# A fused attention and expert kernel on one core: ranks counted back from use in the last part, its last two units interleaved, and early loads planned late

## The chip, the cores and the metric

The kernel runs on one core of one Trainium2 chip. Five engines take part, each with its own queue, worked off in program order: TensorE (PE, with its weight loads shown as PEld), VectorE (DVE), ScalarE (ACT), GpSimd (POOL) and SyncE (SP), which here only issues DMAs. The metric is the device time of one execution in microseconds. It is compared with the median of repeated executions; the profile is that of one execution.

## The reference

```
x = attention(q, k, v)     # 4 batches, 8 heads, 576 positions, 64 wide; scores masked:
                           # heads 0-3 to the last 32 positions, heads 4-7 to every 32nd
x = x.transpose(0, 2, 1, 3).reshape(2304, 512)
p = domain_probs / (domain_probs.sum(-1, keepdims=True) + 1e-9)
for e in range(4):
    h = maximum(x @ w1[e], 0)              # (2304,512) @ (512,1024)
    out += p[:, e:e+1] * (h @ w2[e])       # (2304,1024) @ (1024,512)
```

All arrays are float32.

## The kernel before

**Three parts.** The 2304 rows of x are worked on in three parts of 384, 896 and 1024 rows. The first part runs together with the attention: TensorE takes the small attention products and the expert products of the first 384 rows by turns. The second part (896 rows) and the third (1024 rows) run alone behind it. Each part goes through eight units (four experts, two halves of 512 hidden columns each).

**The precision.** Each float32 operand of an expert product is kept as a high and a low half (`hi`, written by ScalarE; `lo`, the difference, written by VectorE or GpSimd), and each product of two such operands is three matmuls. Every operation here that reads a PSUM bank is VectorE's or ScalarE's.

**The third part.** A unit multiplies in Strassen's manner: 7 products of half-sized blocks for the hidden layer ("h") and 7 for the output ("o"), called P1, P2, s1, s2, s3, s4 and a22. One task, such as "h s2" or "o P1", is a pair of products (two halves f = 0, 1 of the rows of the result, each six matmuls of 128x512 in one PSUM bank, `product`, L897). In `plan_h` the products P1, s2, s3 and a22 accumulate one after the other in the same two ps banks, and s1 and s4 in two mo banks; after each step VectorE reads the bank (`finish`: an add at L928, a relu-and-scale by the expert's probabilities at L931) or ScalarE does (`park`, L919), before the next product may add to it. In `plan_t` the results q are combined (`sub`, L960) and split into halves (`put`: L955 high, L956 low) as the operands of the outputs: b11, t1, t2, b22, t3, b21 and t4 for "o P1", "o s1", "o s2", "o s4", "o s3", "o P2" and "o a22". In `plan_o` P1, s2, s3 and a22 accumulate in two sc banks, s1 and s4 in mo, P2 in ps, and VectorE adds every bank to the sums `acc` (L1005) before the next product goes on in it. Every unit runs through

```
TURN = ("h P1", "h s4", "h s2", "next P2", "h s3", "next s1", "h a22",
        "o P1", "o s1", "o s2", "o s4", "o s3", "o P2", "o a22")
```

where "next" is the hidden product of the unit behind it. Units come in the order 6, 0, 1, 2, 3, 4, 5, 7. The weights of the hidden products come back from DRAM with `reload` (L1033), those of the outputs with `plan_ring` (L983) into a ring of four buffers, all on SP's queue.

**The planner.** `Plan` takes every operation with its engine, its estimated duration, its dependencies and a rank (`prio`, an estimated time). `walk` simulates the engines and writes the program order: whichever engine can start first takes, among the operations that are ready on it, the one of the smallest rank. The expert products (`moe`) keep the order in which they were added; "VP" operations may go to VectorE or GpSimd and "AD" ones to ScalarE or VectorE, wherever they end first. `took` lengthens an operation with two SBUF operands on VectorE by up to half of GpSimd's remaining time. Loads go to SP with a planned wire: each occupies it for its `xfer` time, and `when` says how early an operation may start. Up to 45 us the planner puts idle matmuls (L1205) into gaps. The plan only fixes each engine's order; on the chip every operation waits for its semaphores alone.

The loads of the first part are q and k of a pair of heads (`load_qk`, L418 and L420), v (`load_v`, L425), and the expert weights w1 and w2, one buffer each (`load_w`, L634). A pair's loads are ranked by the planned time of the pair, the weights' by that of their unit; from the fifth pair on they are not planned earlier than 11 us before their use.

Of the kernel before, what the change touches and what calls it, by code (L numbers as in the profile page):

```python
# [11 lines left out]
AF = mybir.ActivationFunctionType  # L12
# [20 lines left out]
class Plan:  # L33
# [5 lines left out]
    TICK = 4096 / 1200  # L39
    BUSY, WARM = 3200, 2000  # L40
    LANES, RING = 8, 2048
    ROW = 2.0
    ENGINES = ("PE", "ACT", "DVE", "POOL", "SP")
    FLEX = {"VP": ("DVE", "POOL"), "AD": ("ACT", "DVE")}
# [59 lines left out]
    def walk(self):  # L104
# [57 lines left out]

        def when(o):
            t = o.ready
            if o.bank:
                n = len(allocs[o.bank[0]]) - self.banks[o.bank[0]]
                if n >= 0:
                    for p in self.readers.get(allocs[o.bank[0]][n], ()):
                        if p.start is None:
                            return None  # L170
                        t = max(t, p.end + self.SYNC)
            return t
# [134 lines left out]
def attn_moe_kernel(  # L307
# [13 lines left out]
    nc = tc.nc  # L321
# [84 lines left out]
    def engine(e):  # L406
        return nc.vector if e == "DVE" else nc.gpsimd
# [498 lines left out]
    DD = TH2 / 960 + 0.15  # L906
    rcnt = [0]

    def plan_h(u, step, z, dz):

        a, b, kk, first_in = STEPS[step]
        PARK = {"P2": "P2", "s1": "k1", "s4": "k2"}
        DONE = {"P1": (0, 0, "P2"), "s2": (0, 1, "k2"), "s3": (1, 1, "k1"), "a22": (1, 0, None)}

        def park(f, key, zz):
            i = ucnt[0] % 6
            ucnt[0] += 1
            late[PARK[step], f] = i
            add("ACT", TH2 / 1200 + 0.18, lambda: nc.scalar.activation(out=late["u"][i], in_=held[key][:, 0:TH2], func=AF.Copy),  # L919
                [key, "late3"], [f"u{i}"], zz)  # L920

        def finish(r, c, nm, f, key, zz):
            tok = f"q{r}{c}{f}"
            q = lambda: late["q"][r, c, f]
            src = lambda: held[key][:, 0:TH2]
            if nm:
                i = late[nm, f]
                add("DVE", DD, lambda: nc.vector.tensor_tensor(out=q(), in0=src(), in1=late["u"][i], op=ALU.add),  # L928
                    [key, f"u{i}", "late3"], [tok], zz)
            from_q = bool(nm)  # L930
            add("DVE", DD, lambda: nc.vector.scalar_tensor_tensor(  # L931
                out=q(), in0=q() if from_q else src(), scalar=0.0, in1=late["p"][:, c * TH2:c * TH2 + TH2], op0=ALU.max, op1=ALU.mult),
                ["pb", "late3"] + ([] if nm else [key]), [tok], zz + 0.1, two=from_q)

        for f in range(2):
            key = ({"a": "ps", "b": "mo", "c": "mo"}[kk], "h" + kk, u, f)
            need = [a + "h", a + "l"] + [f"{b}{h}{j}" for h in "hl" for j in range(2)]
            add("PE", dz, lambda f=f, key=key: product(wq[a], xq[b], f, key, first_in, TH2),
                need, [key], z + f * dz, key if first_in else None, True, 6 * TH2)
            ze = z + f * dz + dz  # L940
            if step in PARK:
                park(f, key, ze)
            else:
                r, c, nm = DONE[step]
                finish(r, c, nm, f, key, ze)

    def plan_t(step, z, dz):


        q = {(r, c, j): (lambda r=r, c=c, j=j: late["q"][r, c, j], f"q{r}{c}{j}") for r in range(2) for c in range(2) for j in range(2)}  # L950

        def put(v, nm, j, zz):
            src, tok = v
            hi, lo = (lambda: late["T"][nm][0][j]), (lambda: late["T"][nm][1][j])
            add("ACT", TH2 / 1200 + 0.17, lambda: nc.scalar.activation(out=hi(), in_=src(), func=AF.Copy), [tok, "late3"], [f"T{nm}h{j}"], zz)  # L955
            add("VP", VP, lambda e: engine(e).tensor_tensor(out=lo(), in0=src(), in1=hi().bitcast(F32), op=ALU.subtract),  # L956
                [tok, f"T{nm}h{j}"], [f"T{nm}l{j}"], zz)

        def sub(dst, a, b, zz):
            add("VP", VP, lambda e: engine(e).tensor_tensor(out=dst[0](), in0=a[0](), in1=b[0](), op=ALU.subtract), [a[1], b[1]], [dst[1]], zz)  # L960

        for j in range(2):
            if step == "P1":
                put(q[0, 0, j], "b11", j, z)
            elif step == "s2":
                sub(q[0, 0, j], q[0, 1, j], q[0, 0, j], z)
                put(q[0, 0, j], "t1", j, z)
            elif step == "s3":
                sub(q[0, 0, j], q[1, 1, j], q[0, 0, j], z)
                put(q[0, 0, j], "t2", j, z)  # L970
                put(q[1, 1, j], "b22", j, z + 2 * dz)
                sub(q[0, 1, j], q[1, 1, j], q[0, 1, j], z + 4 * dz)
                put(q[0, 1, j], "t3", j, z + 4 * dz)
            else:
                put(q[1, 0, j], "b21", j, z + 2 * dz)
                sub(q[1, 0, j], q[1, 0, j], q[0, 0, j], z + 4 * dz)
                put(q[1, 0, j], "t4", j, z + 4 * dz)

    def plan_ring(u, step, z):
        i = rcnt[0] % RING  # L980
# [4 lines left out]
        return i  # L985

    acc_count = {}

    def plan_o(u, step, slot, first, last, z, dz):
        a, b, kk, first_in = STEPS[step]  # L990
        r, c = {"P1": (0, 0), "P2": (0, 0), "s1": (1, 1), "s3": (1, 1), "s2": (0, 1), "s4": (0, 1), "a22": (1, 0)}[step]
        for f in range(2):
            key = ({"a": "sc", "b": "ps", "c": "mo"}[kk], "o" + kk, u, f)
            zz = z + f * dz
            need = [f"ring{slot}"] + [f"T{b}{h}{j}" for h in "hl" for j in range(2)]
            add("PE", dz, lambda f=f, key=key: product(
                [late["ring"][slot][:, :, h] for h in range(2)], late["T"][b], f, key, first_in, TH2),
                need, [key], zz, key if first_in else None, True, 6 * TH2)
            i = (2 * r + f) * 2 + c
            tok = [f"acc{i}0"] if i < TBS[1] // P - 1 else [f"acc{i}{x}" for x in (0, DM // 2)]  # L1000
            n = acc_count[i] = acc_count.get(i, 0) + 1
            if n == 1:
                add("AD", ad(TH2), lambda e, i=i, key=key: copy(e, lambda: acc[i], key, lambda pt: pt[:, 0:TH2]), [key], tok, zz + dz)
            else:
                add("DVE", DD, lambda i=i, key=key: nc.vector.tensor_tensor(  # L1005
                    out=acc[i], in0=held[key][:, 0:TH2], in1=acc[i], op=ALU.add), [key], tok, zz + dz)
            if n == NU * (1 if (r, c) == (1, 0) else 2):
                add("SP", 0.4, lambda i=i, f=f: nc.sync.dma_start(
                    out=out_t[(2 * r + f) * P:(2 * r + f) * P + P, c * TH2:c * TH2 + TH2], in_=acc[i]), tok, [f"out{i}"],
                    zz + dz, xfer=((0.8, 128),))  # L1010
# [11 lines left out]
    def plan_second():  # L1022
# [1 line left out]
        zz = z  # L1024
        seq = second_order
        plan_p(seq[0], zz)
        for step in ("P2", "s1"):
            plan_h(seq[0], step, zz, dz)
            zz += 2 * dz

        def reload(step, v, z):
            nm = STEPS[step][0]
            add("SP", 0.4, lambda: nc.sync.dma_start(out=wt[nm].bitcast(F32), in_=d1[v, nm]), [f"d1{v}{nm}"], [nm + "h", nm + "l"],  # L1033
                z, xfer=((1.45, 128),))

        if NU > 1:
            reload("P2", seq[1], zz)
            reload("s1", seq[1], zz)
        for i, u in enumerate(seq):
            v = seq[i + 1] if i + 1 < NU else None  # L1040
            w = seq[i + 2] if i + 2 < NU else None
            slots = {}
            fetch = list(FETCH)
            for _ in range(RING):
                st = fetch.pop(0)
                slots[st] = plan_ring(u, st, zz)
            for what in TURN:
                kind, step = what.split()
                if kind == "next":
                    if v is None:  # L1050
                        continue
                    plan_h(v, step, zz, dz)
                    if w is not None:
                        reload(step, w, zz + 6 * dz)
                elif kind == "h":
                    plan_h(u, step, zz, dz)
                    if step in ("P1", "s2", "s3", "a22"):
                        plan_t(step, zz + 2 * dz, dz)
                    if v is not None:
                        reload(step, v, zz + 6 * dz)  # L1060
                    if step == "a22" and v is not None and units[v][0] != units[u][0]:
                        plan_p(v, zz + 4 * dz)
                else:
                    plan_o(u, step, slots[step], i == 0, i == NU - 1, zz, dz)
                    if fetch:
                        st = fetch.pop(0)
                        slots[st] = plan_ring(u, st, zz)
                zz += 2 * dz

    ucnt = [0, 0]  # L1070

# [222 lines left out]
```

## Time and profile before

| | |
|---|---|
| median of 3 runs | 824.32 us (823.99 to 825.2) |
| the profiled execution | 825.78 us |
| its span, first to last instruction | 824.0 us |
| mean granted clock of TensorE | 0.995 |
| busy: PE, PEld, DVE, ACT, POOL | 810.3, 686.0, 625.2, 330.6, 308.3 us |
| mean DMA rate | 205 GB/s |

Times in rows count from the start of the span. "Busy" of an engine is the time that its instructions cover; a matmul's own time overlaps the next one's, so of PE the start to start matters. The granted clock is 1.00 at 2.4 GHz and 0.50 at 1.2 GHz. A figure in brackets behind a row is the idle time of the engine just ahead of it, with what released it; "issue" means that the trace shows nothing that was waited for.

### The profile page before, as it was taken

The numbers are of one execution on the slowest core, as the hardware profiler recorded it, in microseconds if no ns is written. First come the engines' busy times: TensorE is split into PE (matmuls) and PEld (weight loads), VectorE is DVE, ScalarE is ACT, GpSimd is POOL, SyncE is SP. The second block draws the span as 40 slices with busy tenths as digits, with TensorE's granted clock in tenths as the row PEclk, the third lists the DMA queues.
The fourth block names the chain that finished last, engine by engine and source line by source line (L and its number), as shares of the span: only waits on it lengthen the run. The fifth ranks groups of instructions, "written<-read, shape, count | busy, mean of one in ns | idle before, by whom it ended". The sixth has DMA issues, their size and how long they took to land.

```text
span 824.0 us, 13898 instructions
## 1 busy us (share of the span) xinstructions
PE 810.3 (98%) x5385; PEld 686.0 (83%) x5388; DVE 625.2 (76%) x892; ACT 330.6 (40%) x616; POOL 308.3 (37%) x243
## 2 busy tenths in 40 slices
PE   8999999999999999999999999999999999999987
PEld 6888888999889888888989888887878787878765
DVE  6877867865588776868677693959796979788886
ACT  4643556444336353543535352524142323323140
POOL 5431332934173542515344270305050505142352
PEclk9999999999999999999999999999999999999998
DMA  9685532339578686867753405747474556635714
GB/s 336 218 312 183 204 138 83 102 125 330 211 256 283 258 307 236 324 212 293 260 205 128 175 30 180 278 157 249 148 251 172 188 211 173 232 125 204 208 48 153
DMA packets 70401, 168.69 MB, mean 205 GB/s; under 512 B 5152, under 2 KB 22720, under 8 KB 70336
## 3 DMA queue, kind: packets, MB, share of 16 engines
q1 hardware_dynamic: 70192, 167.73, 57.5%
q8 instruction: 42, 0.69, 0.3%
q14 instruction: 23, 0.19, 0.1%
q10 hardware_dynamic: 144, 0.08, 0.1%
HBM read 108.00 MB, written 59.79 MB: 204 GB/s over the span
## 4 chain that ended last, share of the span: by engine, by line
PE 95%; DVE 1%; DMA 1%; issue 1%; POOL 1%; ACT 0%; POOLq 0%; ACTq 0%
PE mo L897 21%; PE mo L750 17%; PE ps L897 16%; PE sc L897 15%; PE mo L734 8%; PE ps L750 5%; PE sc L750 5%; PE ps L561 2%; PE sc L479 1%; PE ps L533 1%; PE sc L474 1%; DMA qkL<-in_qk_local 1%; PE ps L569 1%; POOL q L960 1%; PE mo L1205 1%
## 5 line engine op out<-in xcount | busy, mean ns | idle before, releaser
L960 POOL TENSOR_TENSOR q<-q,q 128x512 f32<-128x512 f32 x31 | 44.8, 1445 | 211.9 <-DVE q L931 186.2
L750 PE MATMUL mo<-w2t,h 128*128 128x512 f32 x336 | 80.8, 389 | 0.0
L750 PEld LDWEIGHTS mo<-w2t,h 128*128 128x128 f32 x336 | 63.1, 188 | 13.0
L750 PE MATMUL mo<-w2t,hs 128*128 128x512 f32 x288 | 69.9, 395 | 0.0
L750 PEld LDWEIGHTS mo<-w2t,hs 128*128 128x128 f32 x288 | 53.0, 188 | 11.0
L741 DVE SCALAR_TENSOR_TENSOR h<-c,h 128x448 fp32r<-128x448 f32 x48 | 59.6, 1268 | 2.4 <-ACT h L738 1.0
L645 POOL TENSOR_TENSOR a<-raw,a 128x512 fp32r<-128x512 f32 x22 | 34.1, 1549 | 59.6 <-DVE c L1097 44.9
L644 ACT ACTIVATE w2t<-raw 128x512 fp32r<-128x512 f32 x60 | 36.8, 629 | 37.8 <-PE mo L750 24.7
L1005 DVE TENSOR_TENSOR acc<-sc,acc 128x512 f32<-128x512 f32 x58 | 38.7, 684 | 16.4 <-PE sc L897 15.8
L759 DVE SCALAR_TENSOR_TENSOR acc<-mo,pr,acc 128x512 f32<-128x512 f32 x45 | 33.6, 747 | 22.8 <-PE mo L750 22.5
L928 DVE TENSOR_TENSOR q<-ps,v 128x512 f32<-128x512 f32 x48 | 33.1, 689 | 20.6 <-PE ps L897 20.5
L919 ACT ACTIVATE v<-mo 128x512 f32<-128x512 f32 x48 | 28.7, 598 | 49.5 <-PE mo L897 47.9
L645 POOL TENSOR_TENSOR w2t<-raw,w2t 128x512 fp32r<-128x512 f32 x21 | 30.2, 1447 | 46.6 <-ACT w2t L644 44.0
L734 PE MATMUL mo<-xh,a 128*128 128x384 f32 x192 | 46.7, 345 | 0.0
L955 ACT ACTIVATE Tb11h<-q 128x512 fp32r<-128x512 f32 x16 | 10.0, 627 | 84.5 <-DVE q L931 84.5
L644 ACT ACTIVATE wv<-tmp 128x512 fp32r<-128x512 f32 x32 | 20.1, 631 | 58.0 <-POOL tmp L652 12.8
L931 DVE SCALAR_TENSOR_TENSOR q<-q,pb 128x512 f32<-128x512 f32 x48 | 41.1, 857 | 1.1
L750 PE MATMUL ps<-w2t,h 128*128 128x512 f32 x168 | 40.4, 389 | 0.0
L750 PE MATMUL sc<-w2t,h 128*128 128x512 f32 x168 | 40.4, 389 | 0.0
L645 DVE TENSOR_TENSOR w2t<-raw,w2t 128x512 fp32r<-128x512 f32 x39 | 33.9, 897 | 4.5 <-ACT w2t L644 4.5
L750 PEld LDWEIGHTS sc<-w2t,h 128*128 128x128 f32 x168 | 31.5, 188 | 6.5
L750 PEld LDWEIGHTS ps<-w2t,h 128*128 128x128 f32 x168 | 31.5, 188 | 6.5
(261 smaller groups left out, 2108.0 us busy)
## 6 DMA issues: line engine op xcount, KB each, us to landing
raw<-in_w SPq DMA_DIRECT2D x30, 1024.0 KB, 5.9
qkS<-in_qk_strided SPq DMA_DIRECT2D x16, 329.0 KB, 7.9
vstL<-in_v_local SPq DMA_DIRECT2D x8, 640.0 KB, 8.7
out<-acc SPq DMA_DIRECT2D x18, 256.0 KB, 2.0
vstS<-in_v_strided SPq DMA_DIRECT2D x8, 384.0 KB, 8.7
qkL<-in_qk_local SPq DMA_DIRECT2D x8, 336.0 KB, 6.8
pb<-dp SPq DMA_DIRECT2D x5, 512.0 KB, 6.9
qkL<-in_qk_local SPq DMA_DIRECT2D x8, 272.0 KB, 7.6
```

What stands on the lines that cost most here:

```text
L644: add("ACT", 0.62, lambda: nc.scalar.activation(out=hi(), in_=src(), func=AF.Copy), need, [name + "h"], z)
L645: add("VP", VP, lambda e: engine(e).tensor_tensor(out=lo(), in0=src(), in1=hi().bitcast(F32), op=ALU.subtract), need + [name + "h"], [name ...
L734: nc.tensor.matmul(pt[:, 0:TA], w[:, c % 2, (f % 2) * P:(f % 2) * P + P], (xl if i == 1 else xh)[c], start=j == 0, stop=j == 11)
L741: nc.vector.scalar_tensor_tensor(out=dst(), in0=src(), scalar=0.0, in1=hi().bitcast(F32), op0=ALU.max, op1=ALU.subtract)
L750: nc.tensor.matmul(pt, ht[f][:, ts], wt[f][:, cs], start=j == 0, stop=j == 11)
L759: nc.vector.scalar_tensor_tensor(out=a, in0=pt, scalar=sc, in1=a, op0=ALU.mult, op1=ALU.add)
L897: nc.tensor.matmul(pt, a[i == 2][:, j, f * P:f * P + P], b[i == 1][j][:, 0:TH], start=bool(first) and n == 0, stop=True, skip_group_check= ...
L919: add("ACT", TH2 / 1200 + 0.18, lambda: nc.scalar.activation(out=late["u"][i], in_=held[key][:, 0:TH2], func=AF.Copy), [key, "late3"], [f" ...
L928: add("DVE", DD, lambda: nc.vector.tensor_tensor(out=q(), in0=src(), in1=late["u"][i], op=ALU.add), [key, f"u{i}", "late3"], [tok], zz)
L931: add("DVE", DD, lambda: nc.vector.scalar_tensor_tensor(out=q(), in0=q() if from_q else src(), scalar=0.0, in1=late["p"][:, c * TH2:c * TH ...
L960: add("VP", VP, lambda e: engine(e).tensor_tensor(out=dst[0](), in0=a[0](), in1=b[0](), op=ALU.subtract), [a[1], b[1]], [dst[1]], zz)
L1005: add("DVE", DD, lambda i=i, key=key: nc.vector.tensor_tensor(out=acc[i], in0=held[key][:, 0:TH2], in1=acc[i], op=ALU.add), [key], tok, zz ...
```

## The change

Four things change, all of them in the order that is planned.

In `when`, a transfer that is not planned yet may not start before the planned wire is within DEEP = 1.5 us of being free, as long as the wire stands under 200 us.

In the third part, all tasks of all units are now listed first, and the planned time of every task is kept in `due`. The ranks of `finish`, `put`, `sub` and of the adds to `acc` are counted back from the task that needs their result, instead of on from the task that made it.

Three output tasks of the last unit but one are taken out of their place and put among the hidden tasks of the last unit: "o s3" ahead of its "h s3", "o P2" and "o a22" ahead of its "h a22". For these three, the products of kind b (P2) use mo banks instead of ps.

The ring's loads are planned four output tasks ahead over the whole list, where before every unit planned its first four at its start.

```diff
+    DEEP = 1.5
...
         def when(o):
             t = o.ready
+            if o.xfer is not None and o.start is None and wire < 200:
+                t = max(t, wire - self.DEEP)
...
-                    [key, f"u{i}", "late3"], [tok], zz)
+                    [key, f"u{i}", "late3"], [tok], min(zz, zs) - 0.8)
...
-                ["pb", "late3"] + ([] if nm else [key]), [tok], zz + 0.1, two=from_q)
+                ["pb", "late3"] + ([] if nm else [key]), [tok], zs if nm else min(zz, zs), two=from_q)
...
-                finish(r, c, nm, f, key, ze)
+                after = {"P1": "s2", "s2": "s3", "s3": "a22"}.get(step)
+                use, ops = {"P1": ("P1", 2), "s2": ("s1", 3), "s3": ("s2", 3), "a22": ("P2", 2)}[step]
+                finish(r, c, nm, f, key, due["h", after] + f * dz if after else ze + 4 * dz, due["o", use] - 1.5 - 0.8 * ops - 0.8 + 0.7 * f)
...
-    def plan_t(step, z, dz):
+    def plan_t(step, due):
 ...
-            add("ACT", TH2 / 1200 + 0.17, lambda: nc.scalar.activation(out=hi(), in_=src(), func=AF.Copy), [tok, "late3"], [f"T{nm}h{j}"], zz)
+            add("ACT", TH2 / 1200 + 0.17, lambda: nc.scalar.activation(out=hi(), in_=src(), func=AF.Copy), [tok, "late3"], [f"T{nm}h{j}"], zz - 1.6)
...
-                [tok, f"T{nm}h{j}"], [f"T{nm}l{j}"], zz)
+                [tok, f"T{nm}h{j}"], [f"T{nm}l{j}"], zz - 0.8)
...
+            add("VP", VP, lambda e: engine(e).tensor_tensor(out=dst[0](), in0=a[0](), in1=b[0](), op=ALU.subtract), [a[1], b[1]], [dst[1]], zz - 2.4)
...
+            z = {s: due["o", s] - 1.5 + 0.7 * j for s in STEPS}
...
             elif step == "s3":
-                sub(q[0, 0, j], q[1, 1, j], q[0, 0, j], z)
-                put(q[0, 0, j], "t2", j, z)
-                put(q[1, 1, j], "b22", j, z + 2 * dz)
-                sub(q[0, 1, j], q[1, 1, j], q[0, 1, j], z + 4 * dz)
-                put(q[0, 1, j], "t3", j, z + 4 * dz)
+                sub(q[0, 0, j], q[1, 1, j], q[0, 0, j], z["s2"])
+                put(q[0, 0, j], "t2", j, z["s2"])
+                put(q[1, 1, j], "b22", j, z["s4"])
+                sub(q[0, 1, j], q[1, 1, j], q[0, 1, j], z["s3"])
+                put(q[0, 1, j], "t3", j, z["s3"])
...
+    tags = {"a": "sc", "b": "ps", "c": "mo"}
...
+            after = {"P1": "s2", "s2": "s3", "s3": "a22", "s1": "s4"}.get(step)
+            zd = (due["o", after] + f * dz if after else zz + 5 * dz) - 0.8
...
-                    out=acc[i], in0=held[key][:, 0:TH2], in1=acc[i], op=ALU.add), [key], tok, zz + dz)
+                    out=acc[i], in0=held[key][:, 0:TH2], in1=acc[i], op=ALU.add), [key], tok, zd)
...
+        tasks = [("next", -1, "P2"), ("next", -1, "s1")]
+        for i in range(NU):
             for what in TURN:
                 kind, step = what.split()
...
+                tasks.append((kind, i, step))
+        tasks = [t for t in tasks if t[0] != "next" or t[1] + 1 < NU]
+        late_o = [("o", NU - 2, step) for step in ("s3", "P2", "a22")]
+        tasks = [t for t in tasks if t not in late_o]
+        for t, before in zip(late_o, (("h", NU - 1, "s3"), ("h", NU - 1, "a22"), ("h", NU - 1, "a22"))):
+            tasks.insert(tasks.index(before), t)
+        os = [t for t in tasks if t[0] == "o"]
+        due = [{} for _ in range(NU)]
+        for n, (kind, i, step) in enumerate(tasks):
+            due[i + (kind == "next")][kind[0] if kind != "next" else "h", step] = zz + 2 * dz * n
+        slots = {t: plan_ring(seq[t[1]], t[2], zz) for t in os[:RING]}
+        for t in tasks:
+            kind, i, step = t
+            if kind == "o":
+                tags["b"] = "mo" if t in late_o else "ps"
+                plan_o(seq[i], step, slots[t], i == 0, i == NU - 1, zz, dz, due[i])
+                n = os.index(t) + RING
+                if n < len(os):
+                    slots[os[n]] = plan_ring(seq[os[n][1]], os[n][2], zz)
...
+            zz += 2 * dz
```

The other steps of `plan_t` change as s3 does. The lines for "h" and "next" keep `plan_h`, `plan_t`, `reload` and `plan_p` as they were, with `due` passed on.

## Rows read from the trace of the kernel before

**Rows 1.** The page's first part: busy us, share, instructions of each engine.

```profile
PE 810.3 (98%) x5385; PEld 686.0 (83%) x5388; DVE 625.2 (76%) x892; ACT 330.6 (40%) x616; POOL 308.3 (37%) x243
```

**Rows 2.** Busy time in stretches: stretch, length, engines, granted clock, DMA share, GB/s.

```profile
0.00:40.00 40.00, 36.74 (x696) 28.86 (x700) 30.21 (x72) 21.28 (x48) 20.93 (x34) 1.00 0.77 274
...
60.00:66.00 6.00, 5.52 (x50) 5.26 (x50) 3.07 (x8) 1.65 (x4) 1.08 (x2) 0.72 0.29 116
...
503.34:544.42 41.08, 41.08 (x182) 33.72 (x181) 28.62 (x37) 17.00 (x30) 7.97 (x5) 1.00 0.68 236
544.42:773.24 228.82, 227.40 (x986) 183.79 (x985) 191.12 (x245) 72.36 (x122) 71.98 (x48) 1.00 0.56 194
773.24:820.24 47.00, 43.28 (x181) 34.39 (x179) 35.05 (x48) 9.46 (x16) 15.56 (x10) 0.96 0.36 120
```

**Rows 3.** The chain of waits from 484 us on: start, length, what.

```profile
571.78 0.24 issue
572.01 3.00 PE sc L897 x12
...
580.74 2.72 PE ps L897 x12
583.46 2.72 PE sc L897 x12
...
767.00 0.24 issue
...
804.79 4.56 PE sc L897 x12
```

**Rows 4.** Timeline of all engines, 567 to 578 us: start, length, engine, line.

```profile
570.63 0.68 DVE L931 SCALAR_TENSOR_TENSOR q<-ps,pb 128x512 f32<-128x512 f32 x1
...
571.24 1.27 DVE L1005 TENSOR_TENSOR acc<-sc,acc 128x512 f32<-128x512 f32 x2
...
572.01 0.70 PE L897 MATMUL sc<-Tt2h,ring 128*128 128x512 f32 x2 [0.24 <-issue]
...
572.43 1.35 DVE L956 TENSOR_TENSOR Tb21l<-q,Tb21h 128x512 fp32r<-128x512 f32 x1
...
573.70 0.68 DVE L1005 TENSOR_TENSOR acc<-mo,acc 128x512 f32<-128x512 f32 x1
...
574.30 1.39 DVE L956 TENSOR_TENSOR Tt4l<-q,Tt4h 128x512 fp32r<-128x512 f32 x1
...
575.62 0.68 DVE L1005 TENSOR_TENSOR acc<-mo,acc 128x512 f32<-128x512 f32 x1
...
576.35 0.30 PEld L897 LDWEIGHTS mo<-Tb22h,ring 128*128 128x128 f32 x2 [0.40 <-DVE acc L1005]
```

**Rows 5.** Timeline of all engines, 770 to 824 us.

```profile
795.46 0.73 PE L897 MATMUL ps<-t4h,a 128*128 128x512 f32 x2 [1.52 <-DVE q L928]
...
802.28 1.80 DVE L956 TENSOR_TENSOR Tt2l<-q,Tt2h 128x512 fp32r<-128x512 f32 x1 [1.18 <-ACT Tt2h L955]
...
804.01 0.68 DVE L1005 TENSOR_TENSOR acc<-sc,acc 128x512 f32<-128x512 f32 x1
...
804.79 0.78 PE L897 MATMUL sc<-Tt2h,ring 128*128 128x512 f32 x2 [2.18 <-issue]
```

**Rows 6.** Busy time in stretches of 2 us, columns as in rows 2.

```profile
806.00:808.00 2.00, 2.00 (x6) 1.54 (x6) 2.00 (x4) 0.00 (x0) 1.92 (x2) 0.50 0.00 0
```

**Rows 7.** Instructions of one line: count, then minimum, median and maximum in ns.

```profile
L960 DVE TENSOR_TENSOR q<-q,q x33: 678/694/1779, 517.7 to 806.9; 128x512 f32<-128x512 f32 x33
L960 POOL TENSOR_TENSOR q<-q,q x31: 1283/1295/1752, 523.1 to 807.0; 128x512 f32<-128x512 f32 x31
...
L1005 DVE TENSOR_TENSOR acc<-sc,acc x58: 673/691/693, 540.3 to 820.3; 128x512 f32<-128x512 f32 x58
```

**Rows 8.** SP's timeline up to 230 us: start, length of issue, line.

```profile
10.92 0.38 SPq L634 DMA_DIRECT2D raw<-in_w  x1
```

**Rows 9.** SP's waits, 48 to 70 us: who for whom, total, times, longest.

```profile
SPq L634 <- DVE pmS L488: 13.5, 1, 13.5
```

More of the change, by code (lines that the diff above doesn't have):

```diff
@@ L907, in attn_moe_kernel, with plan_h @@
     rcnt = [0]
-    def plan_h(u, step, z, dz):
+    def plan_h(u, step, z, dz, due):
         a, b, kk, first_in = STEPS[step]
@@ L920, in park, with finish @@
                 [key, "late3"], [f"u{i}"], zz)
-        def finish(r, c, nm, f, key, zz):
+        def finish(r, c, nm, f, key, zz, zs):
             tok = f"q{r}{c}{f}"
@@ L959, in sub @@
         def sub(dst, a, b, zz):
-            add("VP", VP, lambda e: engine(e).tensor_tensor(out=dst[0](), in0=a[0](), in1=b[0](), op=ALU.subtract), [a[1], b[1]], [dst[1]], zz)
+            add("VP", VP, lambda e: engine(e).tensor_tensor(out=dst[0](), in0=a[0](), in1=b[0](), op=ALU.subtract), [a[1], b[1]], [dst[1]], zz - 2.4)
         for j in range(2):
+            z = {s: due["o", s] - 1.5 + 0.7 * j for s in STEPS}
             if step == "P1":
-                put(q[0, 0, j], "b11", j, z)
+                put(q[0, 0, j], "b11", j, z["P1"])
@@ L965, in plan_t @@
             elif step == "s2":
-                sub(q[0, 0, j], q[0, 1, j], q[0, 0, j], z)
-                put(q[0, 0, j], "t1", j, z)
+                sub(q[0, 0, j], q[0, 1, j], q[0, 0, j], z["s1"])
+                put(q[0, 0, j], "t1", j, z["s1"])
             elif step == "s3":
-                sub(q[0, 0, j], q[1, 1, j], q[0, 0, j], z)
-                put(q[0, 0, j], "t2", j, z)
-                put(q[1, 1, j], "b22", j, z + 2 * dz)
-                sub(q[0, 1, j], q[1, 1, j], q[0, 1, j], z + 4 * dz)
@@ L973, in plan_t @@
-                put(q[0, 1, j], "t3", j, z + 4 * dz)
-            else:
-                put(q[1, 0, j], "b21", j, z + 2 * dz)
-                sub(q[1, 0, j], q[1, 0, j], q[0, 0, j], z + 4 * dz)
-                put(q[1, 0, j], "t4", j, z + 4 * dz)
+                sub(q[0, 0, j], q[1, 1, j], q[0, 0, j], z["s2"])
[3 more added lines that the diff above has]
+                put(q[0, 1, j], "t3", j, z["s3"])
+            else:
+                put(q[1, 0, j], "b21", j, z["P2"])
+                sub(q[1, 0, j], q[1, 0, j], q[0, 0, j], z["a22"])
+                put(q[1, 0, j], "t4", j, z["a22"])
@@ L987, in attn_moe_kernel, with plan_o @@
     acc_count = {}
-    def plan_o(u, step, slot, first, last, z, dz):
+    tags = {"a": "sc", "b": "ps", "c": "mo"}
+    def plan_o(u, step, slot, first, last, z, dz, due):
         a, b, kk, first_in = STEPS[step]
@@ L992, in plan_o @@
         for f in range(2):
-            key = ({"a": "sc", "b": "ps", "c": "mo"}[kk], "o" + kk, u, f)
+            key = (tags[kk], "o" + kk, u, f)
             zz = z + f * dz
+            after = {"P1": "s2", "s2": "s3", "s3": "a22", "s1": "s4"}.get(step)
+            zd = (due["o", after] + f * dz if after else zz + 5 * dz) - 0.8
             need = [f"ring{slot}"] + [f"T{b}{h}{j}" for h in "hl" for j in range(2)]
@@ L1002, in plan_o @@
             if n == 1:
-                add("AD", ad(TH2), lambda e, i=i, key=key: copy(e, lambda: acc[i], key, lambda pt: pt[:, 0:TH2]), [key], tok, zz + dz)
+                add("AD", ad(TH2), lambda e, i=i, key=key: copy(e, lambda: acc[i], key, lambda pt: pt[:, 0:TH2]), [key], tok, zd)
             else:
                 add("DVE", DD, lambda i=i, key=key: nc.vector.tensor_tensor(
-                    out=acc[i], in0=held[key][:, 0:TH2], in1=acc[i], op=ALU.add), [key], tok, zz + dz)
+                    out=acc[i], in0=held[key][:, 0:TH2], in1=acc[i], op=ALU.add), [key], tok, zd)
             if n == NU * (1 if (r, c) == (1, 0) else 2):
@@ L1026, in plan_second @@
         plan_p(seq[0], zz)
-        for step in ("P2", "s1"):
-            plan_h(seq[0], step, zz, dz)
-            zz += 2 * dz
         def reload(step, v, z):
@@ L1034, in reload @@
                 z, xfer=((1.45, 128),))
[L1036 to L1046, printed above, removed]
+        tasks = [("next", -1, "P2"), ("next", -1, "s1")]
@@ L1047, in plan_second @@
+        for i in range(NU):
             for what in TURN:
                 kind, step = what.split()
[L1049 to L1067, printed above, removed]
@@ L1068, in plan_second @@
-                zz += 2 * dz
+                tasks.append((kind, i, step))
[6 more added lines that the diff above has]
+        due = [{} for _ in range(NU)]
@@ new lines, in plan_second @@
+        for n, (kind, i, step) in enumerate(tasks):
[9 more added lines that the diff above has]
+                    slots[os[n]] = plan_ring(seq[os[n][1]], os[n][2], zz)
+            else:
+                i += kind == "next"
+                plan_h(seq[i], step, zz, dz, due[i])
+                if step in ("P1", "s2", "s3", "a22"):
+                    plan_t(step, due[i])
+                if i + 1 < NU:
+                    reload(step, seq[i + 1], zz + 6 * dz)
+                    if step == "a22" and units[seq[i + 1]][0] != units[seq[i]][0]:
+                        plan_p(seq[i + 1], zz + 4 * dz)
+            zz += 2 * dz
```

## The prediction

> **What bounds the kernel now.** I read the page first: TensorE is busy 98% of the span, VectorE, the next, 76% [rows 1], so a change that only reorders work can win no more than TensorE's idle time and its time at the lower clock. Next came the table by stretches, to see where those lie [rows 2]: 3.3 us idle in the first 40 us, 0.5 us with a granted clock of 0.72 from 60 to 66 us, and then the last part from 503 us on, whose 112 pairs of products (a pair is 12 matmuls, one task of the written order) should all last the same. They don't. The first 15 pairs take 41.08 us without a gap: 2.739 us a pair. The next 82 pairs (six units of 14, less the two behind 773.24) take 228.82 us, the last 15 take 47.00 us.
>
> The chain of waits says where the middle loses [rows 3]: at every unit, between the pair "o s1" and the pair "o s2", a gap of 0.24 us, then "o s2" in 3.00 instead of the 2.72 us that the pairs behind it take. The same gap stands at 571.78 and 767.00 us, six times in all. VectorE's timeline around the first one names the cause [rows 4]. "o s2" accumulates in the two sc banks that "o P1" filled, and may start only when the add `acc<-sc` has read them; this add starts at 571.24, after a low half of t2 and a relu-and-scale of a22. TensorE starts at 572.01, right behind the first of the two adds. "o s4" has the same wait on the adds of "o s1": they run at 573.70 and 575.62, with a low half of b21 and one of t4 ahead of them, and the weight load goes on at 576.35. Neither b21 nor t4 is wanted before 580.74 and 583.46 [rows 3].
>
> The tail loses more by the same cause [rows 5]: 1.52 us until the add that frees the ps bank of s3, and 2.18 us until t2's low half (it ends at 804.08) and the add behind it (804.69) are done. Then the granted clock is 0.50 [rows 6], 1.2 GHz instead of 2.4, and "o s2" lasts 4.56 us instead of 2.72 [rows 3].
>
> **The ranks (plan_h, plan_t, plan_o).** Nothing is added or taken away: the same matmuls, the same elementwise operations. What changes is the number by which VectorE, GpSimd and ScalarE choose among ready operations. With dz = 1.365 us (six products by the code's own formula) and the unit's first task at 0, the old ranks of the adds of P1 are 15 and 16 dz, 20.5 and 21.8; b22's low halves stand at 16.4, t3 at 19.1, b21 at 21.8, t4 at 24.6; the adds of s1 at 23.2 and 24.6. So b22, t3, and partly b21 rank ahead of adds whose banks are wanted at 18 and 20 dz. The new ranks count back from use: the adds of P1 23.8 and 25.1, b22's low halves 25.0 and 25.7, t3 from 26.1, the adds of s1 26.5 and 27.9, b21 from 30.5, t4 from 31.6. Put into the order of [rows 4]: the first add of P1 passes the second relu-and-scale of a22 (0.61 us from start to start), so it starts at 570.6 and ends at 571.3, before the 571.78 at which "o s1" ends. The adds of s1 pass b21 (1.27 us from start to start) and t4 (1.32): both are over by 574, against 576.3 now. b21 and t4 move back by these two adds, 1.2 us: b21's low half from 573.8 to 575.0, t4's first from 575.7 to 576.9, and are wanted at 580.74 and 583.46, more than 5 us later. So the gaps of all six units go. Worth: 228.82 - 82 x 2.739 = 4.2 us [rows 2]. Lower bound 0 (rival B).
>
> **The moved pairs.** "o s3", "o P2" and "o a22" of the last unit but one move behind "h s2" and "h s3" of the last unit: 6 products, their 6 adds, their ring loads on SP's queue (the ring is now filled four outputs ahead, across units). A pair now stands between s2 and s3, two between s3 and a22. The add that cost 1.52 us has 5.4 us more; from the end of "h s3" to "o s2" it is five pairs, 13.7 us, instead of three. VectorE must do in it: two adds and two products of s3, two subtractions and two low halves of t2, two adds of P1, four moved adds. 14 at 0.69 us [rows 7] are 9.7 us; with t2's four at 1.78, the worst beside GpSimd, 14.0. The first fits well, the second just, because s3's first half is there half a pair (1.4 us) before the second. Banks: the moved P2 goes to mo, whose turn there was last read by a ScalarE copy three pairs earlier; "o P1" of the last unit takes the sc banks of the moved a22, with one pair (2.7 us) between. Those adds are ranked 5 dz - 0.8 = 6.0 us after that task's start and wanted after 5.5, so they may come late by one operation, 0.7 us; I charge that once. Lower bound of this charge 0, upper bound 4.0 us (the tail's second wait and its clock stay). Worth of the move: 47.00 - 41.08 = 5.92 us. The clock comes back with it, since the 2.18 us of idleness ahead of its fall go.
>
> **What the trace says against it.** An elementwise operation with both operands in SBUF lasts 0.68 us alone and up to 1.78 us beside GpSimd; an add that reads PSUM stays within 0.67 to 0.69 [rows 7]. The planner counts at most half of GpSimd's time as delay (`took`), so its order runs ahead of the chip's; if the ranks send more operations to GpSimd, VectorE loses what they give, and that is rival B. The Trainium skill says the same of the ports, more strictly (SBUF — State Buffer, "Who interferes with whom"): such an operation and a GpSimd one that reads SBUF exclude each other, and the loser waits for the whole instruction. By that rule 0.68 + 1.28 = 1.96 us would be the price, an estimate; the longest here is 1.78.
>
> A second rule stands against it: the Trainium skill (Perfetto Trace Analysis, "Optimization Strategy") reads a gap that repeats as a possible lack of SBUF or PSUM for the next tile. By it no order helps, the sc banks being two, and the sum loses its 4.2 us and is rival B's. The trace agrees only half: the wait is for a bank, but the add that frees it starts behind a relu-and-scale of a22 whose result is wanted 10 us later, at 580.74 [rows 3, 4].
>
> **The early loads (DEEP).** In `when`, a load is not planned until the planned wire is within 1.5 us of free, while the wire is under 200 us. No wait is added on the chip: SP still issues in its order, and only the order can change. Up to the second weight load, issued at 10.92 us [rows 8], every load has its buffer from the start, so the choice is by rank with or without the delay: same order, nothing at the head. Behind it SP mostly stands at a weight load whose buffer is not free, 13.5 us at the one near 68 us [rows 9]; the wire is then empty and the new rule idle. What is left are swaps among the few loads of a burst. Bounds: a gain of all that TensorE loses from 60 to 66 us, 0.28 x 6 of clock and 0.48 idle = 2.2 us [rows 2]; a loss of 13.5 us, if a pair's load comes to stand behind such a wait and TensorE needs it at once. Nearest to the rows is 0, which I take.
>
> **Sum.** The profiled execution took 825.78 us: 824.00 of span and 1.78 around it. 825.78 - 4.2 - 5.9 + 0.7 = 816.4. The median of the runs is 1.46 below the profiled execution, which gives 814.9.
>
> **Rivals.**
> A, the forecast: 814.9. Chance 0.60; its own range 813 to 817.
> B, the six gaps stay, because VectorE beside GpSimd is late anyway and the next operation takes the add's place: 825.78 - 1.46 - 5.9 + 0.7 = 819.1. For it: VectorE is busy 191.12 of the 228.82 us [rows 2], and GpSimd makes its operations up to 2.6 times as long. Against it: 16% of its time is free, so the work fits and only the order is wrong. 0.12.
> C, the tail's wait moves instead of closing: the last "o P1" or "o s2" waits about 2 us and the clock falls as before: 814.9 - 0.7 + 2.18 + 1.84 = 818.2. For it: six adds more in the same stretch. 0.12.
> D, slower: one weight load moves ahead of the loads of a pair, SP stands 13.5 us at it as it does now near 68 us, and TensorE, with that pair next in its fixed order, waits for all of it: 814.9 + 13.5 = 828.4. It decides from a stall of about 11 us on. Against it: TensorE has the expert products of the first 384 rows to fill with. 0.05.
> E, the new load order removes the loss at 60 to 66 us as well: 812.7. 0.08.
> F, the new order is in effect the old one on the engines that matter (ranks differ, choices don't) and the moved pairs only move waits: 824.3. 0.03.
>
> **Numbers.** 0.2% (1.6 us) is about what a measurement of this kernel tells from none. A, B, C and E are faster: 0.92; F the same: 0.03; D slower: 0.05. The range takes in A, B, C and E: 812.3 to 819.3.
>
> **What would show it.** In the chain of waits from 503 us on: no "issue" pieces of 0.24, "o s2" and "o s4" at 2.72; units 38.3 us apart instead of 39.04 (767.00 less 571.78 over five). VectorE: `acc<-sc` behind P1 before the low halves of b22 and t4. The last 15 pairs in about 41 to 42 us with the clock at 1.00. SP: the first 15 loads in the old order. I am wrong if a gap of over 0.2 us per unit is left (B), if the clock falls after 770 us (C), or if TensorE's idle time before 140 us differs by more than 1 us from today's (D, E).

## The result, and the profile after

The changed kernel takes 812.05 us (median of 4 runs, 810.9 to 813.96) against 824.76 us (4 runs beside it): a ratio of 0.9845, 95% interval 0.9819 to 0.9872. It is faster, as forecast, but by more: 814.9 was named, with 812.3 as the low end of the range. The profiled execution took 813.96 us, of which 812.1 are its span; before it was 825.78 and 824.0.

The page's first part of the changed kernel stands beside [rows 1]:

```profile
PE 803.2 (99%) x5384; PEld 685.1 (84%) x5388; DVE 603.3 (74%) x860; ACT 326.8 (40%) x615; POOL 351.2 (43%) x276
```

The work is the same, but over the whole span VectorE has 32 instructions fewer and GpSimd 33 more: the new ranks let the planner give GpSimd more. Next the table by stretches, with the third part cut as in [rows 2]: 15 pairs, 82 pairs, 15 pairs.

```profile
40.00:66.00 26.00, 26.00 (x380) 23.14 (x379) 19.72 (x40) 13.20 (x29) 7.53 (x8) 1.00 0.70 257
...
100.00:140.00 40.00, 38.45 (x615) 33.25 (x614) 25.71 (x55) 18.58 (x41) 8.32 (x13) 0.96 0.26 89
112.00:114.00 2.00, 2.00 (x5) 1.61 (x6) 1.14 (x4) 1.09 (x3) 0.43 (x1) 0.50 0.06 14
502.25:543.25 41.00, 41.00 (x182) 33.72 (x181) 28.18 (x33) 16.52 (x29) 15.84 (x10) 1.00 0.69 236
543.25:767.27 224.02, 224.02 (x986) 184.66 (x985) 176.14 (x221) 70.24 (x122) 105.37 (x72) 1.00 0.57 198
767.27:808.34 41.07, 41.06 (x181) 33.45 (x179) 32.25 (x44) 9.69 (x16) 19.95 (x14) 1.00 0.40 137
```

Against [rows 2] the third part gives back 0.08, 4.80 and 5.93 us, 10.81 in all (306.09 instead of 316.90). It also starts 1.09 us earlier, at 502.25 instead of 503.34. TensorE is now idle 0.01 us in it. The idle stretch at 60 to 66 us is gone too, but a new one stands between 100 and 140 us, with the clock at half speed behind it.

The chain of waits through the middle and the tail of the third part, to be held against [rows 3]:

```profile
567.88 2.72 PE mo L900 x12
570.60 2.72 PE sc L900 x12
573.32 2.72 PE mo L900 x12
...
792.01 2.72 PE mo L900 x12
794.73 2.72 PE sc L900 x12
...
805.61 2.73 PE sc L900 x12
```

"o s2" starts at 570.60, right behind "o s1", in 2.72 us instead of 0.24 + 3.00; that of the last unit does so at 794.73, where it waited and lasted 4.56 us before. No pair of the part lasts longer than 2.78, the last 15 included. VectorE's timeline says what stands in the place of [rows 4]:

```profile
566.29 0.68 DVE L961 TENSOR_TENSOR Tt2l<-q,Tt2h 128x512 fp32r<-128x512 f32 x1
566.89 0.68 DVE L1014 TENSOR_TENSOR acc<-sc,acc 128x512 f32<-128x512 f32 x1
567.92 0.69 DVE L1014 TENSOR_TENSOR acc<-sc,acc 128x512 f32<-128x512 f32 x1 [0.35 <-PE sc L900]
568.53 1.40 DVE L961 TENSOR_TENSOR Tb21l<-q,Tb21h 128x512 fp32r<-128x512 f32 x1
569.85 1.48 DVE L1014 TENSOR_TENSOR acc<-mo,acc 128x512 f32<-128x512 f32 x2
```

Both adds of P1 now come ahead of b21's low half, the first right behind one of t2's. The second even waits 0.35 us for TensorE to finish "o P1" (in the chain that pair ends at 567.88): the add waits for the product, no longer the product for the add.

### The profile page after: what moved, and what is told of

Read it like the earlier page. It is cut to its first block, busy times and chain, and to the rows that moved or that the text cites. A ratio compares the mean times of both kernels' runs of the same rounds, so it can differ in the third digit from the quotient of the medians.

```text
span 812.1 us, 13940 instructions
## 1 busy us (share of the span) xinstructions
PE 803.2 (99%) x5384; PEld 685.1 (84%) x5388; DVE 603.3 (74%) x860; ACT 326.8 (40%) x615; POOL 351.2 (43%) x276
## 4 chain that ended last, share of the span: by engine, by line
PE 97%; DMA 2%; DVE 1%; issue 0%; ACT 0%
PE mo L900 22%; PE mo L753 18%; PE ps L900 17%; PE sc L900 15%; PE mo L737 8%; PE ps L753 5%; PE sc L753 5%; PE ps L564 2%; PE sc L482 1%; PE ps L572 1%; PE ps L536 1%; DMA raw<-in_w 1%; PE sc L477 1%; DMA both<-c_masks 0%; DVE wv L648 0%
## 5 line engine op out<-in xcount | busy, mean ns | idle before, releaser
L965 POOL TENSOR_TENSOR q<-q,q 128x512 f32<-128x512 f32 x41 | 60.9, 1492 | 143.5 <-DVE q L934 142.6
L648 POOL TENSOR_TENSOR w2t<-raw,w2t 128x512 fp32r<-128x512 f32 x18 | 26.0, 1447 | 51.2 <-ACT w2t L647 46.9
L965 DVE TENSOR_TENSOR q<-q,q 128x512 f32<-128x512 f32 x23 | 32.7, 1420 | 6.5 <-POOL Tb21l L961 6.2
```

## The experiments

All were timed against the kernel before on the same chip; "third part" is from its first matmul to the end of the last one, in the profile of that kernel (before 316.90, after 306.09).

**1. Is it all in the third part?** The changed kernel without the load rule, and the kernel before with it alone:

```
 t = o.ready
-if o.xfer is not None and o.start is None and wire < 200:
-    t = max(t, wire - self.DEEP)
```

> The changed kernel without the rule for early loads; up to 503 us every engine's order is that of before. If the third part alone carries the gain, as I argued, with no wait left in it: 112 pairs in 306 us instead of 317, so 10.5 to 11 us less than before, and the rest of the change's 12 us is the early loads' (1 to 2 us). Rival, the early loads brought none of it and the scatter of the runs did: the same time as the changed kernel within 0.7 us. Rival, the early loads cost time: faster than the changed kernel.

Measured: 813.34 us, ratio 0.9857 (0.983 to 0.9884); third part 306.01.

> The kernel before with the rule for early loads alone. My prediction took 0 for it: within 1 us of before. Rival, it brings what the sum is short of: 1.5 to 3 us less, with TensorE reaching 140 us of its work earlier by that much. In both cases the third part keeps its six gaps of 0.24 us and its tail of 47.0 us.

Measured: 823.6 us, ratio 0.9985 (0.9966 to 1.0004); third part 316.40, its six gaps unchanged. So the third part's gain comes wholly without the rule. What the rule is worth, these two leave open: without it the changed kernel's median is 1.3 us higher (813.34 against 812.05), with it alone that of the kernel before is 0.5 lower (823.6 against 824.09), both differences that the intervals allow to be nothing.

**2. Ranks alone, and the moved pairs alone.** Neither has the load rule, and both have the fourth change, the ring's loads planned over the whole list, which no run tries by itself. The first has `late_o = []`. The second keeps every old rank (`zz + dz` for the adds, `ze` for `finish`, multiples of dz for `plan_t`) in the new list of tasks.

> New ranks, nothing moved, no rule for early loads. By my steps the six gaps go (4.2 to 4.7 us), and of the tail's 5.9 us a part, since t2 and the adds are ranked ahead there too, but the add that frees s3's bank still has no pair of cover: 5 to 8 us less than before. Rival, the ranks need the moved pairs' cover: under 4 us. Rival, the ranks alone do all: over 10 us.

Measured: 819.5 us, 0.993 (0.9904 to 0.9957). The third part takes 309.98, 6.92 less; the first 97 pairs run without a gap, the tail keeps its waits but not the slow clock. Two stretches of its table, and the chain in the tail:

```profile
502.68:767.62 264.94, 264.94 (x1166) 218.52 (x1165) 204.67 (x254) 86.81 (x151) 121.14 (x82) 1.00 0.59 205
767.62:812.66 45.04, 41.80 (x181) 33.21 (x179) 36.44 (x46) 9.74 (x16) 17.30 (x12) 1.00 0.35 122
```

```profile
794.10 3.37 DVE Tt2l L959 x2
...
798.77 3.00 PE sc L898 x12
```

> The three moved output tasks, and the ring's loads planned over the whole list, with the old ranks; no rule for early loads. By my steps the six gaps of 0.24 us stay, the wait of 1.52 us goes, and the wait of 2.18 us shrinks or goes with its fall of the clock: 4 to 6 us less than before. Rival, with the old ranks the moved adds stand ahead of t2 and the tail waits as long as before: 0 to 2 us less.

Measured: 823.48 us, 0.999 (0.9972 to 1.0008); third part 316.10, only 0.80 less. I expected 4 to 6: that was wrong. Its chain:

```profile
569.52 0.24 issue
569.76 2.97 PE sc L898 x12
...
793.47 2.88 issue
796.35 4.53 PE sc L898 x12
```

The gap of each unit stays, and in the tail "o s2" still waits and still runs at the lower clock, with five pairs in front of it as planned. The time made for VectorE is no use while the order stays: in its timeline the two adds of a moved pair (792.67) and t2's last low half (793.86, 1.78 us long) stand ahead of the adds of P1 (795.57), behind the first of which "o s2" starts at 796.35. Alone the two edits give 6.92 and 0.80, together 10.81: 3.1 us belong to neither.

**3. How much of the ranking is needed?** The kernel before with one number changed, the rank of the adds into `acc`; and the same number in the list of tasks with the moved pairs, the other ranks being those of before:

```
     out=acc[i], in0=held[key][:, 0:TH2], in1=acc[i], op=ALU.add),
-    [key], tok, zz + dz)
+    [key], tok, zz + dz - 10)
```

> The kernel before with one rank changed: the adds of output banks to the sums (L1005) go 10 us ahead of what they were, so VectorE takes each as soon as its bank is full. If the order of these adds is the cause of the six gaps, the gaps of 0.24 us and the slow pairs behind them go, and the 82 pairs take 224 to 224.6 us instead of 228.8; in the tail the adds wait for nobody, but s3's add and t2 are not helped, so the tail keeps 45 to 47 us: 4 to 6 us less in all. Rival, TensorE's wait only moves to t2, which then comes after the adds: under 2 us.

Measured: 815.65 us, 0.9895 (0.9877 to 0.9913); third part 308.27, which is 8.63 less, more than the 4 to 6 expected. No gap is left ahead of 766.96, and the tail keeps one wait, for the adds of s3:

```profile
501.66:766.96 265.30, 265.30 (x1165) 218.25 (x1165) 203.15 (x264) 89.42 (x152) 103.74 (x71) 1.00 0.59 203
766.96:809.93 42.97, 41.41 (x180) 33.26 (x179) 32.82 (x46) 9.59 (x16) 19.03 (x13) 1.00 0.39 132
```

> Old ranks, the three moved pairs, and only the adds into acc ranked 10 us earlier; no load rule. Theory (of the ranks only those of these adds matter, and the moved pairs need them): third part 306 to 307 us without a gap, 813 to 814, that is all of the third part's gain with one rank changed. Rival (the ranks of the halves and of t1 to t4 by due time are needed as well for the moved adds to fit): a wait of 0.5 us or more is left in the last 15 pairs, 307 to 310 us, 814.5 to 817.

Measured: 813.23 us, 0.9869 (0.9854 to 0.9883):

```profile
501.59:807.75 306.16, 306.14 (x1344) 251.88 (x1343) 235.03 (x308) 99.29 (x168) 123.99 (x84) 1.00 0.56 195
```

That is within 0.15 us of the changed kernel's third part, and no piece in the last 15 pairs waits. Of all the new ranks, the one of these adds is enough, given the moved pairs. Without the moved pairs it even does better by itself (8.63) than all the new ranks do (6.92): its tail takes 42.97 us, theirs 45.04. So the one rank brings 4.03 of the tail's 5.93 us, and the moved pairs about 2 more.

**4. Does GpSimd help or hinder?** The changed kernel with all of the third part's subtractions and low halves of `plan_t` on VectorE (`add("DVE", VP[0], ...)` for `add("VP", VP, ...)`).

> The changed kernel with all low halves and subtractions of the third part's outputs on VectorE; GpSimd is idle there. By rival B's mechanism GpSimd's help costs VectorE as much as it gives, so nothing is lost: 50 operations a unit at 0.61 to 0.69 us are 31 to 35 us of 38.3, no gap, the same time within 1 us. Rival, in the stretch from s3 to o s2 VectorE alone has too little time: gaps of over 0.2 us a unit, 1.5 us and more slower.

Measured: 813.44 us, 0.9872 (0.9846 to 0.9898):

```profile
501.06:807.07 306.01, 306.00 (x1344) 251.96 (x1343) 250.21 (x393) 98.94 (x167) 0.00 (x0) 1.00 0.56 195
```

No gap in the third part without GpSimd either. But the median is 1.7 us above that of the changed kernel on the same chip (811.7, experiment 5), more than the 1 us expected, with runs from 811.47 to 816.43. This profile doesn't show why: its third part is as short as any, and where the slowest runs lost their time is not recorded.

GpSimd's 96 instructions in the third part of the changed kernel, 141 us of its time, free only 13.6 us on VectorE (250.21 less 236.57). The instructions of one line say why, first in the changed kernel, then without GpSimd:

```profile
L965 DVE TENSOR_TENSOR q<-q,q x23: 691/1761/1792, 518.1 to 793.7; 128x512 f32<-128x512 f32 x23
```

```profile
L965 DVE TENSOR_TENSOR q<-q,q x64: 681/684/697, 516.2 to 799.0; 128x512 f32<-128x512 f32 x64
```

The median of the subtractions that stay on VectorE is 1.76 us beside GpSimd and 0.68 without it.

**5. The new stall near 110 us.** In the changed kernel's chain:

```profile
108.92 1.28 PE ps L564 x38
110.20 1.54 issue
111.74 0.24 PE ps L564 x2
```

It lies inside a group of small, independent matmuls of the attention, and the chain shows nothing that is waited for. A first guess was the DMA traffic; so the changed kernel was run again, and with the loads of v for the last two pairs of heads cut to their first slice (its output leaves out most of their v).

```
+part = slice(0, 1) if n >= NP - 2 else slice(None)
```

> The changed kernel once more, beside the next two and on their chip. If the rule for early loads is worth 1 us or more, 812 us and a median at least 1 us below the 813.34 of the third part alone; if it is worth nothing, 813 to 814. Its stall of 1.54 us inside the group at L564 near 110 us should stand at the same instruction, of another length.

Measured: 811.7 us, 0.9851 (0.9829 to 0.9873); the same place, only 0.17 us.

> The changed kernel with most of the v loads of the last two pairs left out (a fifth and a half of them are loaded, so those heads' results are wrong); every engine's order is the changed kernel's. TensorE stalls near 110 us after the same 38 of 40 matmuls while the DMA engines are fully busy. If the load on the DMA engines makes the stall, it goes or is under 0.3 us, the clock stays at 1.00, and the time is 1.5 to 3 us below the changed kernel's. Rival, the stall belongs to that place of the program whatever the transfers do: 1.0 to 1.5 us again.

Measured: 811.88 us, 0.9849 (0.9828 to 0.9869); the same place, 0.45 us. Fewer bytes neither took the stall away nor saved time: the guess found no support.

The traces show what it most likely waits for, among the DMA queues (queue, packets, MB, share of 16 engines). First the whole span of the changed kernel, then 57.50 to 58.00 us of the kernel before, then 109.00 to 109.50 of the changed one:

```profile
q8 instruction: 42, 0.69, 0.3%
...
q8 instruction: 1, 0.02, 12.6%
...
q8 instruction: 1, 0.02, 13.3%
```

A queue named "instruction" brings 42 packets of 16 KB, one for about every 256 of TensorE's 10772 matmuls and weight loads (an estimate from the counts). One packet is under way from 109.21 to 110.28, just ahead of the stall that ends at 111.74; the kernel before has one from 57.98 to 58.98 ahead of its stall near 60 us, which ends at 60.48. In all thirteen profiles the stall ends 1.36 to 1.53 us after such a packet does, the seventh packet without the load rule and the fifteenth with it, and the two places lie 2047 entries apart in TensorE's queue (matmuls, weight loads and waits), eight times 256 less one. I read from this that TensorE waits there for its own next instructions: on the chip an operation does not wait for its semaphores alone. No run changed these packets, so why one comes late is open; this one takes about 1 us, like the others.

**6. What the load rule is worth.** The changed kernel without it and with it, on one chip:

> The changed kernel without the load rule, once more, beside the changed kernel itself on the same chip. Theory (the rule is worth what E's first part says, the stall and the slow clock at 60 to 66 us traded for a smaller stall near 110 us): 0.5 to 1.6 us slower than the kernel with the rule by the medians, third part 306.0 us in both, the difference wholly ahead of the third part. Rival (the rule is worth nothing, as the prediction had it): medians within 0.4 us of each other.

Measured: 813.6 us (4 runs, 813.14 to 814.79), 0.9876 (0.9861 to 0.989).

> The changed kernel itself, timed beside the one without the load rule. Theory (the rule is worth 0.5 to 1.6 us): median 811.0 to 812.5, and below that of the kernel without it by that much; TensorE runs 60 to 66 us without a piece marked issue and stalls 0.2 to 1.5 us near 110 us. Rival (worth nothing): median 812.5 to 813.5, as the one without.

Measured: 811.94 us (4 runs, 811.03 to 812.58), 0.9855 (0.9838 to 0.9871). The two sets of runs don't overlap, and the medians are 1.66 us apart: the rule is worth that. (Single runs of other sets do overlap, but over all 13 runs of the changed kernel and all 9 without the rule the medians are 811.70 and 813.34.) Both third parts take 306.01 us; the one with the rule starts at 499.56, the other at 501.58. But the cause that I had named isn't it. Up to 500 us TensorE is idle equally long in these two profiles, 4.58 us without the rule (first line) and 4.56 with it, and the clock is 1.00 in both:

```profile
sum 500.00, PE 495.42 PEld 431.20 DVE 370.76 ACT 231.66 POOL 213.16; mean PE 99.08 PEld 86.24 DVE 74.15 ACT 46.33 POOL 42.63
sum 500.00, PE 495.44 PEld 432.05 DVE 366.38 ACT 230.58 POOL 211.39; mean PE 99.09 PEld 86.41 DVE 73.28 ACT 46.12 POOL 42.28
```

What differs is how long the same matmuls keep TensorE busy. Groups by line and shape up to 499 us (count, busy us, mean ns, idle before), without the rule:

```profile
L735 PE MATMUL mo<-xh,a 128*128 128x384 f32 x192 | 46.1, 342 | 0.0
L562 PE MATMUL ps<-pTL,vstL 64*64 64x32 f32 x576 | 18.1, 221 | 0.4 <-issue 0.4
L480 PE MATMUL sc<-qkS 64*64 64x54 f32 x384 | 14.5, 221 | 0.7 <-issue 0.7
L475 PE MATMUL sc<-qkL 64*32 64x63 f32 x576 | 11.2, 222 | 0.4 <-DMA qkL<-in_qk_local 0.4
L534 PE MATMUL ps<-ident,pmS 128*128 128x128 f32 x48 | 7.9, 280 | 0.3 <-DVE xl L613 0.3
```

and with it:

```profile
L737 PE MATMUL mo<-xh,a 128*128 128x384 f32 x192 | 45.6, 341 | 0.0
L564 PE MATMUL ps<-pTL,vstL 64*64 64x32 f32 x576 | 17.8, 221 | 1.2 <-issue 1.0
L482 PE MATMUL sc<-qkS 64*64 64x54 f32 x384 | 14.8, 221 | 0.4 <-DMA qkS<-in_qk_strided 0.4
L477 PE MATMUL sc<-qkL 64*32 64x63 f32 x576 | 10.4, 217 | 0.3 <-DVE pmS L491 0.3
L536 PE MATMUL ps<-ident,pmS 128*128 128x128 f32 x48 | 7.2, 276 | 0.2
```

These five groups, the ones of the first part that differ by 0.3 us or more (idle filler matmuls aside), sum to 97.8 and 95.8 us, and 2.0 us is what the third part starts earlier. These times count twice where one matmul overlaps the next; from start to start and without idle time, the matmuls ahead of the second part take 207.72 and 205.64 us, and of that difference 1.4 us are in the five groups, the rest mostly in the products of L570 and in one idle filler matmul more. The same sum of five groups parts all the other profiles: 97.2 to 98.3 in the seven without the rule, 95.8 to 96.4 in the six with it (that of before, 98.3, has some of them at the lower clock). Why a matmul takes more or less room shows in the chain without the rule:

```profile
76.39 1.39 PE mo L751 x6
77.78 0.33 PE ps L534 x3
78.10 0.84 PE sc L480 x24
78.94 0.48 PE ps L534 x3
```

Three transposes take 0.33 us behind an expert product and 0.48 behind small attention products; the same two figures stand at 70.28 and 71.30 us. The rule, by delaying loads in the plan, changes how the planner mixes the two kinds. That the mix makes the whole difference is argued from this: no run changed it alone.

## Why the prediction was right in direction and short in size

**The gaps of the six units** (worth 4.2): right in mechanism. They close by the order of the adds into `acc`, and by that alone, as experiment 3 shows with one rank changed. Measured 4.80. The term was 0.6 short because the price of a pair was taken from the first 15 pairs (2.739 us), one of which lasts 2.82 (at 541.60); the 82 pairs now take 2.732 each. The other rule weighed against this, that a gap which repeats can mean too few buffers (the Trainium skill, Perfetto Trace Analysis, "Optimization Strategy"), does not hold here: with the same two sc banks and one number changed, the gap is gone.

**The moved pairs** (worth 5.92, less 0.7): the total is right, the attribution is not. The 5.92 came, 5.93 measured. But the one rank of experiment 3, without the move, already takes the tail from 47.00 to 42.97 us, and the move without ranks wins 0.8. So that the 5.92 came out is partly luck. I priced them as two terms that add; they are an order and the room for it, and the room is worth little without the order. The charge of 0.7 for one late add was not needed: no pair of the tail exceeds 2.78.

**The early loads** (taken at 0, between a gain of 2.2 and a loss of 13.5): this is the step that failed. "Nearest to the rows is 0, which I take" should have been about 1.6 gained. My rival E had the sign, at a chance of 0.08, and with 812.7 the nearest number, but not for its reason: the stall near 60 us went and another came, and the idle time stayed. "Same order, nothing at the head" held for SP's queue, where the traces (without the rule and with it, experiments 1 and 5) show the same kinds of loads up to the 45th, not for the other engines: VectorE and ScalarE differ from their 6th instruction on, and of TensorE's matmuls the 83rd is already another. The rule delays SP's loads in the plan, and with them every operation that waits for them there. And my bounds priced only idle time and clock, while the gain is in the busy time of the same matmuls.

**The sum.** 0.7 not needed, 0.6 more from the gaps and 1.66 from the rule make 2.96 us; 814.9 less 812.05 is 2.85.

**The signs named.** No gap of 0.24, "o s2" and "o s4" at 2.72, the clock at 1.00 in the last 15 pairs and 41.07 us for them: all as forecast. The order named for VectorE came only in part: the adds of P1 do run ahead of t4's low halves, but those of b22 (561.67 on VectorE, 564.59 on GpSimd) ran ahead of the adds all the same, before the product was done, and the adds of s1 (569.85) passed only one of b21's two. It did not matter, since no pair waits. TensorE's idle time in the first 140 us differs by 0.35 us (4.78 now, 4.43 before), under the 1 us that I gave as the sign of D or E; so that sign could not see what the rule does.

**The rivals.** B (VectorE beside GpSimd is late anyway) and C (the tail's wait moves) fell. B's ground is real, an operation with both operands in SBUF lasts up to 1.79 us beside GpSimd (1.80 before, at 802.28 in [rows 5]; the prediction took 1.78 for the longest), but it did not decide: without GpSimd the third part takes the same 306.01 us. D, a stall of 13.5 us, does not appear; F fell.

## What to carry to other kernels

When an engine is nearly always busy, look for the short gap that repeats, and read what its releasing engine did just before: if that was work wanted much later, the first thing to change is the order on that engine, and here one rank gave 8.6 of 10.8 us. Price two edits of one queue together, since room in a queue is worth little (here 0.8 us) until the urgent work goes first. And where a change lets a planner mix small and large matmuls anew, expect the busy time itself to move, not only the gaps.

## What the runs showed of the hardware that had not been expected

**A stall behind a packet of instructions.** In every order without the load rule TensorE stops once between two identical matmuls of one group near 60 us (L479 before, 12 instructions into it); with the rule this stall is gone, and one stands at 38 of 40 matmuls of another group near 110 us. The place is the same in every execution of an order, the length is not: 0.75, 0.47, 0.75, 0.35, 0.73, 0.47 and 0.47 us in the seven profiles without the rule, 1.54, 1.00, 0.17, 0.45, 0.93 and 1.00 us in the six with it. It ends 1.36 to 1.53 us after a packet of the "instruction" queue (experiment 5), which fits the place: the order decides which matmuls stand where the next packet is needed. Why the packet comes late stays open: the DMA share just ahead of the stall is about 1.0 in both places (0.99 in the 2.2 us before 110.20 of the changed kernel), but fewer bytes left it standing.

**The clock behind it.** The granted clock fell to about 0.50 (1.2 GHz) behind this stall in four of the thirteen profiles, and not only behind the longest: of two stalls of 1.00 us, one was followed by a fall and one was not. With the stall's length this makes most of the difference between two executions of one order: the third part of the changed kernel, always 306.0 to 306.1 us long, started at 502.25 in one profile (stall 1.54, clock 0.50 behind it) and at 499.22 in another (0.17, clock 1.00).

**GpSimd's help is worth little here.** In the third part, 141 us of work on GpSimd spare VectorE 13.6 us, and without GpSimd the profiled third part is no longer; the higher median of those runs (experiment 4) stays unexplained.
